# Two phase-weight loads given other landing buffers, and one tile's turn and store moved to other engines, in a chunk-attention and phase-MLP kernel

## The chip, the cores and the metric

The kernel runs on one core of a Trainium2 chip. The metric is the device time of one execution in microseconds (us). Three runs of the kernel before took 190.2, 190.77 and 191.58 us, with a median of 190.77 us. One further execution was profiled, and it took 190.93 us.

## The reference

Eight batches of 576 tokens pass through attention with 8 heads of 64 features, each chunk of 64 tokens attending only to itself. The 512 features of each token then go through a phase layer, a token mix and a channel layer.

```python
scores = scale * np.matmul(q_c, k_c.transpose(0, 1, 2, 4, 3))   # chunks of 64
attn = softmax(scores)
x = np.matmul(attn, v_c)                                        # heads side by side: (8, 576, 512)
theta = x @ w_theta
zr, zi = x * np.cos(theta), x * np.sin(theta)
u = x + np.einsum('ts,bsd->btd', w_tok_r, zr) + np.einsum('ts,bsd->btd', w_tok_i, zi)
out = u + np.maximum(u @ w_ch, 0.0)
```

## The kernel before, in words

The batches are handled in four pairs p = 0 to 3. A batch has 4 full tiles of 128 tokens and a half tile of 64; the two halves of a pair share one tile. So a pair has nine tiles j = 0 to 8, and j = 8, the middle tile (`MID`), holds the last 64 tokens of both batches. Loads and attention go by groups: A and B are the two pairs of tiles of the first batch, C and D those of the second, M is the middle tile.

Nothing plans the order of the work: it is written out by hand in the list `ORDER` (lines 17 to 64), and a loop at the end (lines 640 to 647) issues it step by step. Each engine takes its own instructions of that list strictly in turn. A step reads `kind.pg.slot`: the kind names a function of the table `work` (lines 612 to 639), then come pair and group (or pair and tile), then a buffer or a PSUM bank. Whoever takes a buffer again waits until its former content has been read, by a DMA too: a step that writes an output buffer `o` again waits until the store out of it has landed. The steps that this text speaks of are:

- `hq.0A`, `hk.0A` (`load_qk32`, line 180): q and k of group 0A as 32-bit floats by SP's DMA queue, 512 KB each, into landing buffers 0 and 1. `cqa.0A` on ScalarE (ACT) and `ckv.0A` on VectorE (DVE) cast them into landing buffer 3 (line 192).
- `lt.00`, `lt.01` (`load_theta`, line 252): the two halves of `w_theta`, 512 KB each, also by SP's queue. `cta.01` and `cta.00` (line 261) cast them on ACT. TensorE (PE) needs both before `H0.0A`, the first product with `w_theta`.
- `qk` (line 161) and `v` (line 205): all other loads of q, k and v. They are issued by GpSimd (POOL), which casts them to 16 bits on the way.
- `Tq`, `Tk`, `T` (line 314) turn q and k in 32 x 32 blocks on DVE; `S` and `V` are the products of attention on PE; `E` the exponentials on ACT; `dm.n` are n matmuls of zeros on PE, which fill its waits (line 155).
- `Y` mixes tokens on PE (line 523); `A` adds x on DVE (line 550), which makes u.
- u must be turned before the channel product. `U` does it with four transposes on PE into a PSUM bank (line 554), and `ua` copies the bank into a buffer `uT` on ACT. `ud` does it as one DMA transpose from SP's queue into `uT` (line 565).
- `W` is the channel product on PE (line 575): four matmuls of 512 columns. `R` takes relu and adds u on DVE, into a buffer `o` (line 588).
- Stores of `o` (line 600): `st` from SP's queue, `sa` from ACT's, `sg` from POOL's. A middle tile takes two DMAs of 64 rows, one per batch. `sx` issues the first of these on SP and the second on ACT; the table has it, but `ORDER` before doesn't use it.

Near the end, `ORDER` writes the buffers `o` in this order (the last number is the buffer): `R.35.1 R.31.2 R.34.0 R.30.3 R.36.5 R.33.1 R.27.2 R.32.4 R.38.0 R.24.3 R0.37.1 R1.37.2`. Out of these, ACT stores 35, 34, 33, 27, 24 and the second half of the columns of 37, in that order. So `R.33` waits for the store of 35 (both use `o` 1), `R0.37` for the store of 33 (`o` 1) and `R1.37` for the store of 27 (`o` 2).

Of the kernel before, what the change touches and what calls it, by code (L numbers as in the profile page):

```python
# [19 lines left out]
V1.0A.6 N0.0A S.0M.0 N1.0A cta.01 Tq.0B.2 E.0M.1 v.0M cta.00 dm.6.3 X1.0A.2 Tk0.0B  # L20
X0.0A.3 dm.2.7 S0.0B.4 Tk1.0B V0.0M.0 xa0.0A.0 V1.0M.1 xa1.0A N0.0M E0.0B.2 S1.0B.6
E1.0B H0.0A.3 v.0B V1.0B.4 G0.0A.0 V0.0B.6 lw.01.7 H1.0A.2 N1.0M N1.0B X.0M.0 xa.0M.1
lw.03.8 N0.0B TW.01.4 twv.01 X1.0B.1 X0.0B.3 lw.02.9 xv0.0B.2 lw.00.10 G1.0A Z0.0A Z1.0A
xa1.0B H.0M.6 G.0M.1 H0.0B.7 TW.03.4 G0.0B.2 H1.0B.0 twv.03 G1.0B Z.0M Z0.0B qk.0C.11
Ya.01.3 v.0C Z1.0B TW.02.1 qk.0D.12 Ya.03.6 twa.02 Tq.0C.0 TW.00.4 Ym.05.7 Tk.0C v.0D
Ya.02.0 Yb.02 twv.00 S.0C.1 Ym.02 A.02 Yb.01 E.0C.3 Ym.01 V1.0C.4 A.01 V0.0C.0 Tq.0D.1
N1.0C Yb.03 lc.00 Ya.00.2 U.02.3 Tk.0D Yb.00 Ym.00 S.0D.4 N0.0C ua.02.0 A.00 X.0C.3
U.00.0 U.01.1 Ym.03 E.0D.0 xv.0C.3 uv.01.1 V1.0D.4 ua.00.2 N1.0D V0.0D.2 N0.0D qk.1M.0
qk.1A.1 H.0C.0 v.1M qk.1B.3 A.03 v.1A Ym.06.4 X.0D.5 W.02.2 Ym.07.3 xv.0D.0 G.0C.0 Z.0C
H.0D.5 Ya.05 Ya.06 Ya.07 G.0D.1 T.1M.2 S.1M.0 T.1A.0 Z.0D R.02.0 S.1A.5 E.1A.1 Yb.05  # L30
Yb.06 Ym.04.2 A.05 E.1M.2 V0.1M.5 N0.1M qk.1D.5 V1.1M.6 V1.1A.0 A.06 N1.1M Ya.04 T.1B.1
Yb.07 U.06.7 ua.06.3 A.07 X.1M.5 Yb.04 xa.1M.1 S.1B.6 N1.1A lw.04.4 TW.04.4 twv.04
H.1M.3 A.04 v.1B V0.1A.0 E.1B.3 V1.1B.4 G.1M.2 qk.2A.2 V0.1B.6 N0.1A N0.1B N1.1B Y.08.2
A.08 X.1A.0 W.00.1 U.04.6 qk.1C.6 X.1B.7 xa.1A.2 R.00.1 qk.2M.7 Z.1M T.1D.2 xa.1B.3
qk.2B.8 v.1D U.08.3 ua.08.4 v.2M v.1C ua.04.5 H.1A.4 G.1A.0 st.02 H.1B.0 W.08.2 W.06.7
U.05.3 T.1C.0 S.1D.4 G.1B.1 qk.2C.9 Z.1A Z.1B ua.05.6 E.1D.0 S.1C.0 W.01.6 R.06.2 U.07.3
sa.06 E.1C.2 T.2A.1 ua.07.7 Y.12.7 V1.1D.4 R.01.3 V0.1D.0 Y.13.6 T.2M.2 N0.1D S.2M.0
sa.01 E.2M.1 R.08.4 N1.1D S.2A.2 V1.1C.4 E.2A.3 sa.08 V0.1C.0 A.12 Y.11.7 X.1D.2 xa.1D.0
N1.1C N0.1C X.1C.3 xv.1C.1 Y.10.4 A.13 H.1D.0 qk.3M.10 v.2B T.2C.0 A.11 A.10 T.3M.2
G.1D.2 Z.1D H.1C.2 W.04.5 R.04.5 U.03.6 W.05.7 S.2C.0 v.2A st.00 S.3M.4 uv.03.0 G.1C.0  # L40
Z.1C R.05.0 E.3M.0 v.3M E.2C.2 st.04 V1.2A.2 N1.2A W.03.6 R.03.1 T.2B.1 Y.16.7 A.16
V0.2M.4 N0.2M v.2C V1.2C.2 V1.2M.5 qk.3A.11 N1.2C S.2B.0 N1.2M E.2B.1 qk.2D.12 Y.18.6
V1.3M.7 V0.2C.0 A.18 N0.2C V0.2B.2 N0.2B Y.14.4 V1.2B.5 V0.2A.0 qk.3C.0 v.2D N1.2B
U.18.2 Y.15.3 X.2B.5 A.14 X.2M.6 W.07.4 uv.18.2 xa.2B.2 N0.2A xa.2M.3 A.15 X.2A.2 v.3B
xa.2A.0 H.2B.0 T.3C.0 R.07.2 T.2D.2 G.2B.1 qk.3B.1 W.18.3 R.18.3 H.2A.5 U.15.4 Y.17.2
U.10.3 H.2M.0 Z.2B G.2A.2 ua.15.4 ua.10.3 N1.3M G.2M.0 S.3C.5 Z.2A A.17 S.2D.3 E.2D.2
W.15.1 U.17.7 Z.2M Y.20.2 uv.17.1 V1.2D.3 E.3C.1 A.20 V0.3M.0 V0.2D.5 st.05 Y.23.7
xd.2C.1 N1.2D A.23 N0.2D T.3B.1 U.14.2 U.11.3 sa.18 N0.3M xd.2D.2 W.17.4 ua.11.5 U.16.7
R.15.4 st.07 Y.21.3 A.21 R.17.5 qk.3D.3 v.3C v.3A H.2C.5 ua.16.6 T.3A.0 W.10.7 ua.14.0
G.2C.1 T.3D.2 H.2D.0 G.2D.2 Y.22.2 Z.2C R.10.0 S.3D.3 S.3A.5 st.15 E.3A.3 S.3B.0 E.3D.0  # L50
Z.2D Y.26.7 sg.03 U.12.5 A.22 U.13.2 sa.10 ua.13.7 W.11.6 R.11.3 Y.25.3 A.26 E.3B.2 v.3D
sa.11 ud.23.2 ud.21.4 W.16.4 A.25 R.16.1 W.13.2 V1.3D.0 R.13.2 V1.3A.6 V0.3A.3 N1.3D
ua.12.1 N0.3A st.16 sa.13 xd.3M.0 N1.3A Y.24.5 A.24 Y.27.2 A.27 W.12.0 R.12.4 V0.3D.3
V1.3B.6 V0.3B.1 N1.3B xd.3A.3 ud.20.3 N0.3B N0.3D Y.28.5 V1.3C.6 V0.3C.0 A.28 W.14.2
H.3M.3 G.3M.0 R.14.0 xd.3B.1 ud.25.5 N0.3C H.3A.4 xd.3D.2 G.3A.1 W.21.2 N1.3C R.21.3
W.23.0 Z.3A H.3B.6 G.3B.2 sg.17 Z.3M ud.24.6 W.25.1 sa.21 R.23.5 xd.3C.0 H.3D.2 ud.28.7
W.20.4 H.3C.5 ud.22.1 G.3D.1 R.25.1 Z.3B Y.30.0 G.3C.0 Z.3D ud.26.0 sg.12 Z.3C Y.31.7
R.20.2 A.30 A.31 Y.36.1 Y.35.2 W.22.3 A.35 R.22.4 Y.33.5 W.28.6 A.33 Y.34.4 sg.23 A.34
ud.35.4 R.28.3 ud.31.2 W.26.0 Y.32.7 Y.37.2 W.35.3 A.36 ud.33.5 R.26.5 W.31.5 A.32 A.37
# [618 lines left out]
```

## Time and profile before

| what | value |
|---|---|
| median of three runs | 190.77 us (190.2 to 191.58) |
| the profiled execution | 190.93 us |
| its span, first to last instruction | 189.2 us |
| PE busy | 180.9 us (96%), 2645 matmuls |
| DVE busy | 136.7 us (72%) |
| ACT busy | 94.8 us (50%) |
| POOL busy | 89.5 us (47%) |
| matmuls of zeros (line 157), part of PE's | 51, 14.1 us |
| DMA moved | 31.48 MB, mean 166 GB/s |

Times in the profile count from the span's first instruction. "PE" is TensorE's matmuls and "PEld" its weight loads, which overlap them; "SPq" and "ACTq" are DMAs issued by those engines' queues. In a row of the timeline the first number is the start, the second the duration (of several instructions that follow each other, their common stretch), and brackets tell how long the engine was idle before and what ended that.

### The profile page before, as it was taken

The page shows a single profiled execution, that of the slowest core. Times are in us where ns is not written, and L with a number is a line of the kernel's source. Part 1 is how long each engine was busy: PE and PEld are TensorE (multiplying, and loading weights), DVE is VectorE, ACT ScalarE, POOL GpSimd, SP SyncE. Part 2 cuts the span into 40 slices and gives each one's busy share as a digit, 9 for nine tenths or more (in the row PEclk, how much of TensorE's full clock was granted, in tenths as well). Part 3 has the DMA queues.
Part 4 walks back from the last instruction along what each step waited for, and adds up shares of the span by engine and source line. Part 5 has one row for each costly group of instructions (what it writes and reads, how often), then busy time and mean ns, then how long its engine had stood idle before and what let it go on. Part 6 is the DMA issues. An engine that isn't in the chain of part 4 may idle for free.

```text
span 189.2 us, 6104 instructions
## 1 busy us (share of the span) xinstructions
PE 180.9 (96%) x2645; PEld 93.4 (49%) x2645; DVE 136.7 (72%) x259; ACT 94.8 (50%) x123; POOL 89.5 (47%) x129
## 2 busy tenths in 40 slices
PE   7998999999999999999999999999999999999970
...
GB/s 151 285 194 172 177 167 170 189 168 168 192 194 180 198 126 206 178 101 191 209 166 146 172 214 52 248 60 59 140 153 154 183 177 59 55 110 204 206 317 166
DMA packets 99227, 31.48 MB, mean 166 GB/s; under 512 B 90880, under 2 KB 94848, under 8 KB 99200
## 3 DMA queue, kind: packets, MB, share of 16 engines
...
q1 hardware_dynamic: 20896, 8.92, 21.2%
...
## 4 chain that ended last, share of the span: by engine, by line
PE 74%; DMA 17%; DVE 3%; issue 2%; POOL 2%; SPq 0%; DVEq 0%; POOLq 0%
PE psum L540 34%; PE psum L475 15%; PE psum L580 12%; DMA land<-in_k_dram 9%; PE psum L354 4%; PE psum L400 3%; DMA land<-in_q_dram 3%; DMA uT<-x 3%; PE psum L437 2%; PE psum L557 2%; DMA v<-in_v_dram 2%; PE psum L287 2%; POOL v L213 1%; DVE o L592 1%; DVE T L335 1%
## 5 line engine op out<-in xcount | busy, mean ns | idle before, releaser
L213 POOL DMA_DIRECT2D v<-in_v_dram x56 | 41.7, 765 | 14.5 <-DMA land<-in_k_dram 9.1
L540 PEld LDWEIGHTS <-wT 128*128 128x128 f16 (+1 forms) x360 | 30.6, 100 | 33.4 <-issue 0.8
L540 PE MATMUL psum<-zr,wT 128*128 128x512 f16 (+1 forms) x180 | 45.4, 381 | 0.1
L540 PE MATMUL psum<-zi,wT 128*128 128x512 f16 (+1 forms) x180 | 43.1, 379 | 0.0
L608 POOL DMA_DIRECT2D out_dram<-o x10 | 5.5, 552 | 66.3 <-DVE o L592 46.2
L580 PE MATMUL psum<-wch,uT 128*128 128x512 f16 (+1 forms) x148 | 35.2, 374 | 1.1 <-DMA uT<-x 1.1
L552 DVE TENSOR_TENSOR x<-psum,x 128x512 f16<-128x512 f32 x36 | 24.4, 683 | 15.8 <-PE psum L540 15.1
L475 PE MATMUL psum<-wtheta,xT 128*128 128x512 f16 x144 | 34.1, 379 | 0.0
L592 DVE SCALAR_TENSOR_TENSOR o<-psum,x 128x512 f32<-128x512 f32 (+1 forms) x37 | 24.3, 670 | 10.3 <-PE psum L580 6.2
L494 ACT ACTIVATE cos<-psum,pihalf 128x1024 f16<-128x1024 f32 (+1 forms) x22 | 21.2, 964 | 16.1 <-PE psum L475 16.1
L335 DVE STREAM_TRANSPOSE T<-land 64x256 f32<-64x256 f32 (+3 forms) x38 | 27.0, 725 | 2.6 <-DMA land<-in_k_dram 2.3
L417 DVE TENSOR_TENSOR x<-psum,recip 128x512 f16<-128x512 f32 (+1 forms) x40 | 25.5, 638 | 1.4
L383 ACT ACTIVATE eT<-psum 128x1024 f16<-128x1024 f32 (+1 forms) x22 | 18.4, 864 | 15.8 <-PE psum L354 15.8
L580 PEld LDWEIGHTS <-uT 128*128 128x128 f16 x148 | 13.7, 98 | 16.2 <-DMA uT<-x 1.6
L475 PEld LDWEIGHTS <-xT 128*128 128x128 f16 x144 | 13.5, 98 | 15.3 <-DVE xT L460 0.2
...
L494 ACT ACTIVATE sin<-psum 128x1024 f16<-128x1024 f32 (+1 forms) x22 | 19.1, 870 | 0.0
L173 POOL DMA_DIRECT2D land<-in_q_dram x15 | 13.6, 904 | 4.8 <-DVE recip L415 2.1
L157 PE MATMUL psum<-zeros 128*128 128x512 f16 x51 | 14.1, 436 | 1.2 <-DVE pihalf L148 1.2
L173 POOL DMA_DIRECT2D land<-in_k_dram x15 | 13.5, 902 | 2.0 <-DMA land<-in_k_dram 1.4
L462 ACT COPY xT<-psum 128x512 f16<-128x512 f16 (+1 forms) x11 | 8.4, 784 | 10.4 <-PE psum L437 10.4
L354 PEld LDWEIGHTS <-T 32*64 32x64 f16 x1152 | 10.6, 105 | 5.4 <-DVE T L335 2.1
...
## 6 DMA issues: line engine op xcount, KB each, us to landing
land<-in_q_dram POOLq DMA_DIRECT2D x15, 256.0 KB, 6.8
land<-in_k_dram POOLq DMA_DIRECT2D x15, 256.0 KB, 7.8
out_dram<-o ACTq DMA_DIRECT2D x12, 256.0 KB, 3.2
...
out_dram<-o POOLq DMA_DIRECT2D x10, 256.0 KB, 3.4
out_dram<-o SPq DMA_DIRECT2D x9, 256.0 KB, 3.3
...
```

Source lines behind the costliest of these rows:

```text
L173: nc.gpsimd.dma_start(t[:, w].rearrange("p h s d -> p h (s d)"), ap[2 * p + bb, :, s0 : s0 + GT, :].rearrange("h (p s) d -> p h (s d)", s=2),)
L213: nc.gpsimd.dma_start(v16[rows, slot + t, :, 0:D], v[b, :, t0 : t0 + m, :].rearrange("h s d -> s h d"),)
L335: nc.vector.transpose(to.bitcast(FP32).rearrange("p (x l s) -> p x s l", l=32, s=2), src.bitcast(FP32).rearrange("p (x s d) -> p x s d", s ...
L354: nc.tensor.matmul(ps[half[rows], r, h - hs[0]], t[quarter[c], 1, h, :, e], t[quarter[c], 0, h, :, e], start=(e == 0), stop=(e == 1), tile ...
L383: nc.scalar.activation(out=to, in_=ps, func=AF.Exp, scale=scale)
L417: nc.vector.tensor_tensor(out=x.rearrange("p r (h d) -> p r h d", h=H // 2), in0=ps[:, :, :, 0:D], in1=recip[:, 0:n].broadcast_to((P, n, H ...
L475: nc.tensor.matmul(ps[:, (j - js[0]) * DM : (j - js[0] + 1) * DM], xT[:, j, a, :], wtheta16[:, a, :], start=(a == 0), stop=(a == NDB - 1),)
L494: nc.scalar.activation(out=t[:, js[0] : js[-1] + 1].rearrange("p j e -> p (j e)"), in_=ps, func=AF.Sin, bias=bias, scale=1.0,)
L540: nc.tensor.matmul(ps[half[c]] if j == MID else ps, wT[:, kt, t0 : min(t0 + P, S)], z, start=(b is not None and i == 0), stop=(i == len(kt ...
L552: nc.vector.tensor_tensor(out=x, in0=st.pop(("ps_y", p, j)), in1=x, op=ALU.add)
L580: nc.tensor.matmul(ps, uT[:, a, :], wch16[:, a, cols[f]], start=(a == 0), stop=(a == NDB - 1),)
L592: nc.vector.scalar_tensor_tensor(out=o, in0=ps, scalar=0.0, in1=st["x", p][:, j, cols[f]], op0=ALU.max, op1=ALU.add,)
```

## The change

Only `ORDER` changes. Nothing is added to the functions.

1. `lt.00` goes into landing buffer 0 instead of 2 and stands behind `cqa.0A`; `lt.01` goes into buffer 1 instead of 4 and stands behind `ckv.0A`. Each load therefore waits, on SP's queue, until the cast has read the buffer.
2. The turn of u of tile 38 (the middle tile of the last pair) is `U.38.2 ua.38.3` behind `W.36` instead of the DMA transpose `ud.38.3` behind `ud.37`. In ACT's own queue `ua.38` now stands ahead of `sa.35`, and so of all later stores of ACT.
3. The store of tile 38 is `sx.38` ahead of `W.24` instead of `st.38` behind `R0.37`. Its first half is issued by SP, its second by ACT ahead of `sa.24`.

In the list (lines are wrapped anew from the first changed one on, so the parts are cut out; the code below `ORDER` stands three lines higher afterwards):

```diff
-pre.00 hq.0A.0 hk.0A.1 lt.00.2 cqa.0A.3 ckv.0A Tq.0A.0 init.00 Tk1.0A Tk0.0A dm.28.7
-S0.0A.0 S1.0A.2 lt.01.4 qk.0M.5 E0.0A.0 v.0A dm.15.7 V0.0A.4 E1.0A Tq.0M.1 Tk.0M qk.0B.6
+pre.00 hq.0A.0 hk.0A.1 cqa.0A.3 lt.00.0 ckv.0A lt.01.1 Tq.0A.0 init.00 Tk1.0A Tk0.0A dm.28.7
+S0.0A.0 S1.0A.2 qk.0M.5 E0.0A.0 v.0A dm.15.7 V0.0A.4 E1.0A Tq.0M.1 Tk.0M qk.0B.6 V1.0A.6 N0.0A
 ...
-ud.27.4 sg.14 W.34.6 W.36.1 W.30.0 W.33.7 sg.31 sa.35 R.34.0 ud.37.2 ud.38.3 R.30.3
-st.30 W.27.2 sa.34 R.36.5 sg.22 R.33.1 sg.36 R.27.2 W.32.3 R.32.4 W.38.5 R.38.0 sg.32
-sa.33 sa.27 W.24.4 R.24.3 sa.24 W0.37.6 R0.37.1 st.38 W1.37.0 R1.37.2 sa1.37 st0.37
+ud.27.4 sg.14 W.34.6 W.36.1 U.38.2 ua.38.3 W.30.0 W.33.7
+sg.31 sa.35 R.34.0 ud.37.2 R.30.3 st.30 W.27.2 sa.34 R.36.5 sg.22 R.33.1 sg.36 R.27.2 W.32.3
+R.32.4 W.38.5 R.38.0 sg.32 sa.33 sa.27 sx.38 W.24.4 R.24.3 sa.24 W0.37.6 R0.37.1 W1.37.0 R1.37.2
+sa1.37 st0.37
```

More of the change, by code (lines that the diff above doesn't have):

```diff
@@ L17 @@
 ORDER = """
-pre.00 hq.0A.0 hk.0A.1 lt.00.2 cqa.0A.3 ckv.0A Tq.0A.0 init.00 Tk1.0A Tk0.0A dm.28.7
-S0.0A.0 S1.0A.2 lt.01.4 qk.0M.5 E0.0A.0 v.0A dm.15.7 V0.0A.4 E1.0A Tq.0M.1 Tk.0M qk.0B.6
[L20 to L59, printed above, removed]
@@ L60 @@
-Y.38.4 ud.34.3 ud.30.1 st.26 ud.36.7 sa.20 sg.25 sa.28 R.35.1 R.31.2 ud.32.0 A.38
-ud.27.4 sg.14 W.34.6 W.36.1 W.30.0 W.33.7 sg.31 sa.35 R.34.0 ud.37.2 ud.38.3 R.30.3
-st.30 W.27.2 sa.34 R.36.5 sg.22 R.33.1 sg.36 R.27.2 W.32.3 R.32.4 W.38.5 R.38.0 sg.32
-sa.33 sa.27 W.24.4 R.24.3 sa.24 W0.37.6 R0.37.1 st.38 W1.37.0 R1.37.2 sa1.37 st0.37
+pre.00 hq.0A.0 hk.0A.1 cqa.0A.3 lt.00.0 ckv.0A lt.01.1 Tq.0A.0 init.00 Tk1.0A Tk0.0A dm.28.7
+S0.0A.0 S1.0A.2 qk.0M.5 E0.0A.0 v.0A dm.15.7 V0.0A.4 E1.0A Tq.0M.1 Tk.0M qk.0B.6 V1.0A.6 N0.0A
@@ new lines @@
+S.0M.0 N1.0A cta.01 Tq.0B.2 E.0M.1 v.0M cta.00 dm.6.3 X1.0A.2 Tk0.0B X0.0A.3 dm.2.7 S0.0B.4
+Tk1.0B V0.0M.0 xa0.0A.0 V1.0M.1 xa1.0A N0.0M E0.0B.2 S1.0B.6 E1.0B H0.0A.3 v.0B V1.0B.4 G0.0A.0
+V0.0B.6 lw.01.7 H1.0A.2 N1.0M N1.0B X.0M.0 xa.0M.1 lw.03.8 N0.0B TW.01.4 twv.01 X1.0B.1 X0.0B.3
+lw.02.9 xv0.0B.2 lw.00.10 G1.0A Z0.0A Z1.0A xa1.0B H.0M.6 G.0M.1 H0.0B.7 TW.03.4 G0.0B.2 H1.0B.0
+twv.03 G1.0B Z.0M Z0.0B qk.0C.11 Ya.01.3 v.0C Z1.0B TW.02.1 qk.0D.12 Ya.03.6 twa.02 Tq.0C.0
+TW.00.4 Ym.05.7 Tk.0C v.0D Ya.02.0 Yb.02 twv.00 S.0C.1 Ym.02 A.02 Yb.01 E.0C.3 Ym.01 V1.0C.4
@@ new lines @@
+A.01 V0.0C.0 Tq.0D.1 N1.0C Yb.03 lc.00 Ya.00.2 U.02.3 Tk.0D Yb.00 Ym.00 S.0D.4 N0.0C ua.02.0
+A.00 X.0C.3 U.00.0 U.01.1 Ym.03 E.0D.0 xv.0C.3 uv.01.1 V1.0D.4 ua.00.2 N1.0D V0.0D.2 N0.0D
+qk.1M.0 qk.1A.1 H.0C.0 v.1M qk.1B.3 A.03 v.1A Ym.06.4 X.0D.5 W.02.2 Ym.07.3 xv.0D.0 G.0C.0 Z.0C
+H.0D.5 Ya.05 Ya.06 Ya.07 G.0D.1 T.1M.2 S.1M.0 T.1A.0 Z.0D R.02.0 S.1A.5 E.1A.1 Yb.05 Yb.06
+Ym.04.2 A.05 E.1M.2 V0.1M.5 N0.1M qk.1D.5 V1.1M.6 V1.1A.0 A.06 N1.1M Ya.04 T.1B.1 Yb.07 U.06.7
+ua.06.3 A.07 X.1M.5 Yb.04 xa.1M.1 S.1B.6 N1.1A lw.04.4 TW.04.4 twv.04 H.1M.3 A.04 v.1B V0.1A.0
@@ new lines @@
+E.1B.3 V1.1B.4 G.1M.2 qk.2A.2 V0.1B.6 N0.1A N0.1B N1.1B Y.08.2 A.08 X.1A.0 W.00.1 U.04.6 qk.1C.6
+X.1B.7 xa.1A.2 R.00.1 qk.2M.7 Z.1M T.1D.2 xa.1B.3 qk.2B.8 v.1D U.08.3 ua.08.4 v.2M v.1C ua.04.5
+H.1A.4 G.1A.0 st.02 H.1B.0 W.08.2 W.06.7 U.05.3 T.1C.0 S.1D.4 G.1B.1 qk.2C.9 Z.1A Z.1B ua.05.6
+E.1D.0 S.1C.0 W.01.6 R.06.2 U.07.3 sa.06 E.1C.2 T.2A.1 ua.07.7 Y.12.7 V1.1D.4 R.01.3 V0.1D.0
+Y.13.6 T.2M.2 N0.1D S.2M.0 sa.01 E.2M.1 R.08.4 N1.1D S.2A.2 V1.1C.4 E.2A.3 sa.08 V0.1C.0 A.12
+Y.11.7 X.1D.2 xa.1D.0 N1.1C N0.1C X.1C.3 xv.1C.1 Y.10.4 A.13 H.1D.0 qk.3M.10 v.2B T.2C.0 A.11
@@ new lines @@
+A.10 T.3M.2 G.1D.2 Z.1D H.1C.2 W.04.5 R.04.5 U.03.6 W.05.7 S.2C.0 v.2A st.00 S.3M.4 uv.03.0
+G.1C.0 Z.1C R.05.0 E.3M.0 v.3M E.2C.2 st.04 V1.2A.2 N1.2A W.03.6 R.03.1 T.2B.1 Y.16.7 A.16
+V0.2M.4 N0.2M v.2C V1.2C.2 V1.2M.5 qk.3A.11 N1.2C S.2B.0 N1.2M E.2B.1 qk.2D.12 Y.18.6 V1.3M.7
+V0.2C.0 A.18 N0.2C V0.2B.2 N0.2B Y.14.4 V1.2B.5 V0.2A.0 qk.3C.0 v.2D N1.2B U.18.2 Y.15.3 X.2B.5
+A.14 X.2M.6 W.07.4 uv.18.2 xa.2B.2 N0.2A xa.2M.3 A.15 X.2A.2 v.3B xa.2A.0 H.2B.0 T.3C.0 R.07.2
+T.2D.2 G.2B.1 qk.3B.1 W.18.3 R.18.3 H.2A.5 U.15.4 Y.17.2 U.10.3 H.2M.0 Z.2B G.2A.2 ua.15.4
@@ new lines @@
+ua.10.3 N1.3M G.2M.0 S.3C.5 Z.2A A.17 S.2D.3 E.2D.2 W.15.1 U.17.7 Z.2M Y.20.2 uv.17.1 V1.2D.3
+E.3C.1 A.20 V0.3M.0 V0.2D.5 st.05 Y.23.7 xd.2C.1 N1.2D A.23 N0.2D T.3B.1 U.14.2 U.11.3 sa.18
+N0.3M xd.2D.2 W.17.4 ua.11.5 U.16.7 R.15.4 st.07 Y.21.3 A.21 R.17.5 qk.3D.3 v.3C v.3A H.2C.5
+ua.16.6 T.3A.0 W.10.7 ua.14.0 G.2C.1 T.3D.2 H.2D.0 G.2D.2 Y.22.2 Z.2C R.10.0 S.3D.3 S.3A.5 st.15
+E.3A.3 S.3B.0 E.3D.0 Z.2D Y.26.7 sg.03 U.12.5 A.22 U.13.2 sa.10 ua.13.7 W.11.6 R.11.3 Y.25.3
+A.26 E.3B.2 v.3D sa.11 ud.23.2 ud.21.4 W.16.4 A.25 R.16.1 W.13.2 V1.3D.0 R.13.2 V1.3A.6 V0.3A.3
@@ new lines @@
+N1.3D ua.12.1 N0.3A st.16 sa.13 xd.3M.0 N1.3A Y.24.5 A.24 Y.27.2 A.27 W.12.0 R.12.4 V0.3D.3
+V1.3B.6 V0.3B.1 N1.3B xd.3A.3 ud.20.3 N0.3B N0.3D Y.28.5 V1.3C.6 V0.3C.0 A.28 W.14.2 H.3M.3
+G.3M.0 R.14.0 xd.3B.1 ud.25.5 N0.3C H.3A.4 xd.3D.2 G.3A.1 W.21.2 N1.3C R.21.3 W.23.0 Z.3A H.3B.6
+G.3B.2 sg.17 Z.3M ud.24.6 W.25.1 sa.21 R.23.5 xd.3C.0 H.3D.2 ud.28.7 W.20.4 H.3C.5 ud.22.1
+G.3D.1 R.25.1 Z.3B Y.30.0 G.3C.0 Z.3D ud.26.0 sg.12 Z.3C Y.31.7 R.20.2 A.30 A.31 Y.36.1 Y.35.2
+W.22.3 A.35 R.22.4 Y.33.5 W.28.6 A.33 Y.34.4 sg.23 A.34 ud.35.4 R.28.3 ud.31.2 W.26.0 Y.32.7
```

2 lines of the change are left out of this document (added).

## The prediction

> **What bounds the kernel now.** I read the page first, then PE's waits, the chain, and the timelines of the first 20 and last 20 us.
>
> ```profile
> span 189.2 us, 6104 instructions
> PE 180.9 (96%) x2645; PEld 93.4 (49%) x2645; DVE 136.7 (72%) x259; ACT 94.8 (50%) x123; POOL 89.5 (47%) x129
> ...
> PE   7998999999999999999999999999999999999970
> ...
> L157 PE MATMUL psum<-zeros 128*128 128x512 f16 x51 | 14.1, 436 | 1.2 <-DVE pihalf L148 1.2
> ```
>
> ```profile
> PE psum L157 <- DVE pihalf L148: 1.2, 1, 1.2
> PE psum L580 <- DMA uT<-x: 1.1, 1, 1.1
> PE psum L354 <- DVE T L335: 0.8, 1, 0.8
> ```
>
> The second view lists all waits of PE, each with its total, count and longest. PE waits three times only: 1.2 us at the start, 0.8 us for turned q and k, and 1.1 us for a turned u. From the second wait to the third it runs without a gap, so what comes earlier or later at the front moves everything behind it. The change touches the last two. Their places:
>
> ```profile
> 9.72 0.71 PE L354 MATMUL psum<-T 32*64 32x64 f16 x64
> 10.36 3.41 PE L157 MATMUL psum<-zeros 128*128 128x512 f16 x15
> ...
> 17.66 0.45 PE L354 MATMUL psum<-T 32*64 32x64 f16 x32 [0.81 <-DVE T L335]
> ```
>
> ```profile
> 7.76 9.38 DMA land<-in_k_dram
> 17.14 0.02 issue
> 17.16 0.46 DVE T L335
> ...
> 52.58 0.22 PE psum L557 x4
> ...
> 176.01 5.32 DMA uT<-x
> ```
>
> The first fence is PE's timeline, the second the chain of waits. The wait at 17.66 (`S0.0B`) ends with k of group 0B, which POOL issued at 7.76 and which landed at 17.14. The wait at the end is for `ud.38`, issued at 176.01 and landed at 181.33.
>
> **Part 1, the theta loads.** Cost by the rows, ACT's, DVE's and SP's timeline:
>
> ```profile
> 5.13 1.04 ACT L199 CAST land<-land 128x1024 f16<-128x1024 f32 x1 [2.89 <-DMA land<-in_q_dram]
> ...
> 11.20 1.05 ACT L265 CAST wtheta<-land 128x1024 f16<-128x1024 f32 x1
> 14.59 0.60 ACT L383 ACTIVATE eT<-psum 128x512 f16<-128x512 f32 x1 [2.34 <-PE psum L354]
> 15.09 1.04 ACT L265 CAST wtheta<-land 128x1024 f16<-128x1024 f32 x1
> ```
>
> ```profile
> 7.11 0.69 DVE L201 CAST land<-land 128x1024 f16<-128x1024 f32 x1 [5.32 <-DMA land<-in_k_dram]
> ```
>
> ```profile
> 1.87 1.95 SPq L256 DMA_DIRECT2D land<-in_moe_w_theta_dram  x2
> ```
>
> `lt.00` is issued at about 6.2 (5.13 + 1.04) instead of 1.87, `lt.01` at about 7.85 (7.11 + 0.69) instead of some 3.3. On SP's queue nothing stands behind them until the stores, much later, so the waits there block nobody. The loads of q and k stood ahead of the theta loads in the same queue, so I don't expect them to land earlier. If they did, PE would still work through its 28 matmuls of zeros up to 9.72.
>
> How late may theta be? Landing took 7.5 to 7.7 us where the loads stood behind q and k, while those two, on an empty queue, took 4.4 and 5.8 us:
>
> ```profile
> L256 SPq DMA_DIRECT2D land<-in_moe_w_theta_dram x2: 471/955/1439, 1.9 to 3.3; - x2
> ...
> DMA to landing us min/median/max: 7.5/7.6/7.7
> ```
>
> ```profile
> L185 SPq DMA_DIRECT2D land<-in_q_dram x1: 451/451/451, 0.7 to 0.7; - x1
> L185 SPq DMA_DIRECT2D land<-in_k_dram x1: 567/567/567, 1.3 to 1.3; - x1
> ...
> DMA to landing us min/median/max: 4.4/5.1/5.8
> ```
>
> The queue is nearly empty now, so I take 4.4 to 5.8: `lt.01` lands between 12.3 and 13.7, `cta.01` moves from 11.20 to there and ends by 14.75. Behind it in ACT's queue stands the exponential of 14.59, so this is free within 0.2 us. With 7.7 it would land at 15.55; `cta.01`, the exponential, `cta.00`, two copies (1.07) and the exponentials of 0B would follow one another, and `V1.0B` would start some 0.7 us late. That is the upper bound.
>
> Does k of 0B land earlier? POOL issued it behind seven loads, and its bytes, theta's and those ahead of it must all pass by 17.14 either way. The DMA engines carry as much before 6 us as after:
>
> ```profile
> 3.00:4.00 1.00, 1.00 (x4) 0.34 (x3) 0.00 (x0) 0.00 (x0) 1.00 (x3) 1.00 1.14 345
> ...
> 7.00:8.00 1.00, 1.00 (x6) 0.49 (x5) 0.89 (x2) 0.00 (x0) 0.41 (x2) 1.00 1.14 280
> 8.00:9.00 1.00, 1.00 (x7) 0.41 (x6) 1.00 (x4) 0.00 (x0) 0.64 (x1) 1.00 1.22 321
> ```
>
> (the last two numbers of a row of windows are the DMA engines' share and GB/s). They are full throughout; moving theta 1.5 us later in that stream changes the order, not the sum. So I take 0, between a gain of 0.81 (the whole wait) and a loss of 0.7.
>
> **Part 2, the turn of tile 38.** The tail, PE's, DVE's, ACT's and SP's timelines:
>
> ```profile
> 174.92 5.35 PE L580 MATMUL psum<-wch,uT 128*128 128x512 f16 x24
> 181.37 2.77 PE L580 MATMUL psum<-wch,uT 128*128 128x512 f16 x16 [1.10 <-DMA uT<-x]
> ```
>
> ```profile
> 175.03 0.69 DVE L552 TENSOR_TENSOR x<-psum,x 128x512 f16<-128x512 f32 x1 [1.38 <-PE psum L540]
> ...
> 177.72 3.28 DVE L592 SCALAR_TENSOR_TENSOR o<-psum,x 128x512 f32<-128x512 f32 x5 [1.03 <-PE psum L580]
> 182.45 0.69 DVE L592 SCALAR_TENSOR_TENSOR o<-psum,x 128x512 f32<-128x512 f32 x1 [1.45 <-PE psum L580]
> 183.31 1.35 DVE L592 SCALAR_TENSOR_TENSOR o<-psum,x 128x512 f32<-128x512 f32 x3 [0.17 <-PE psum L580]
> ```
>
> ```profile
> 172.82 12.29 ACTq L608 DMA_DIRECT2D out_dram<-o  x6
> ```
>
> ```profile
> 183.17 1.19 SPq L605 DMA_DIRECT2D out_dram<-o  x2
> 184.46 0.53 SPq L608 DMA_DIRECT2D out_dram<-o  x1
> ```
>
> The 24 matmuls are `W` of 34, 36, 30, 33, 27, 32, the 16 are 38, 24 and both halves of 37. The five of DVE are `R` of 30, 36, 33, 27, 32, some 0.6 apart, so `R.33` starts at about 178.92; then come `R.38` and, in the last row, `R.24`, `R0.37` and `R1.37`, the last starting at 184.25 and ending at 184.66. The six stores of ACT are 35 (at 172.82), 34, 33, 27, 24 and the second half of 37.
>
> PE gains the 1.10 us and pays 0.22 (four transposes, as at 52.58 in the chain): W of 38 starts at about 180.4, and PE ends at 183.2 instead of 184.14, 0.9 us earlier. `A.38` ends at 175.72, before `U.38` can start (`W.36` leaves PE at 174.92 + 8 x 0.216 = 176.65), and `ud.37`, due at 182.1, landed at 180.02. By PE alone this part gains 0.9.
>
> But `ua.38` is queued on ACT ahead of `sa.35`. A copy of this kind took:
>
> ```profile
> L569 ACT COPY uT<-psum x2: 586/586/586, 128.1 to 130.1; 128x512 f16<-128x512 f16 x2
> ```
>
> The four transposes have left PE at about 177.03, the copy lasts until 177.66, and `sa.35` is issued at about 177.75 instead of 172.82: 4.9 us later. `sa.34` follows it, and its reader `R.38` is not due before 181.5. `R.33`, however, writes the buffer out of which `sa.35` stores, and may start only when that has landed; behind it on DVE stand `R.27`, `R.32`, `R.38`, `R.24` and both halves of `R.37`. And these take buffers again themselves: `R1.37` waits for the store of `R.27`. With d for a store's time from issue to landing, `R.33` starts at 177.80 + d; `R.27` 0.60 later, ends 0.68 later still; `sa.27` is issued 0.03 behind, lands after d, and `R1.37` starts 0.05 later. The sum: `R1.37` starts at 179.16 + 2d. The rows for d:
>
> ```profile
> out_dram<-o ACTq DMA_DIRECT2D x12, 256.0 KB, 3.2
> ```
>
> ```profile
> L608 ACTq DMA_DIRECT2D out_dram<-o x6: 338/338/413, 172.8 to 184.7; - x6
> ...
> DMA to landing us min/median/max: 2.6/3.3/4.4
> ```
>
> The first is the median of all of ACT's stores of this size, the second the six at the end alone. With 3.2, `R.33` starts at 181.0 (2.1 us late), and `R1.37` at 185.56 instead of 184.25: 1.3 us later. With 2.6 it is 184.36 (0.1 later), with 4.4 it would be 187.96 (3.7 later). I take 3.2, because the stores around the same moment (issued from 176.7 to 180.6) had 3.4 and 4.4, but with two DMA transposes beside them, one of which goes.
>
> [...]
>
> **Part 3, the store of 38 in halves.** SP issued two DMAs in 1.19 us, so `st0.37` went out at 184.46, 0.1 behind them. Now one leaves from each queue, and earlier than `R0.37`. `st0.37` then goes directly behind its `R0.37`, at 185.0 + 0.4 by the sum above, ahead of `sa1.37`, which stays last. ACT's extra issue (0.34 in the rows of ACT's stores) comes before `R1.37` ends, so it is free. With the stores of 38 and 24 out of the way over 1 us ahead of the last one I give it 0.2 us back of its landing; between 0 and the distance from 3.3 to 2.6, that is 0.7.
>
> **The sum.** 0 at the front, +1.3 by the reuse of `o`, -0.2 at the last landing: +1.1 us. The profiled execution took 190.93 us, 1.7 more than its span of 189.2; so 192.0 for it. Its time stands 0.16 above the median of the three runs, which makes 191.9 us against 190.77.
>
> **The rivals.**
>
> *Faster, because stores land quickly.* `R1.37` starts earlier than before if 179.16 + 2d is below 184.25, that is with d below 2.55. For it speaks that `ud.38` no longer competes and that `sa.35` is the first of a new burst; against it that five of the six rows lie above and none below 2.6. With 2.4 the tail gains 0.3, and 190.5 comes out. Should nobody wait for `o` at all, PE's 0.9 would count: 189.9.
>
> *Slow landings.* With `sa.35`, `sa.34` and the stores of SP and POOL leaving within 2 us, d may be as in the worst row, 4.4: 3.7 later, 194.5 us. For it: the two rows of 4.4 and 3.4 at this very moment.
>
> *The front pays.* If k of 0B lands 0.8 earlier, `S0.0B` doesn't wait, and all behind it gains 0.81: 191.1. If theta is the later one, 0.7 is lost: 192.6. Neither changes the sign.
>
> *The change doesn't do what it says.* With d at 2.6 PE's gain and the new wait cancel out: 190.9.
>
> **How the numbers follow.** The forecast (d of 2.8 to 3.7) has 0.53, the fast landings 0.12, the cancelling 0.17, slow landings 0.18; the front shifts each by up to 0.8 and is as likely either way. The predicted time is 191.9; its own range is 191.0 to 193.0. The range for 8 of 10 leaves out half of the fast case and the worst of the slow one: 190.3 to 193.6. Within 1% is 188.9 to 192.7, about what a measurement of this kernel can tell from no change. Faster by more takes the whole of PE's gain and the front's together: 0.04. Slower by more takes d above 3.6 or a loss at the front: 0.25. The rest, 0.71, is within 1%.
>
> **What would show it.** Right: the copy of tile 38 on ACT at about 177.1 with `sa.35` directly behind it, a wait of about 2 us of DVE ahead of the third of the five `R`, released by a store; PE's wait of 1.1 us gone and PE done near 183.2; `R1.37` starting near 185.5; the wait of 0.8 at 17.66 still there. Wrong: DVE not waiting for a store in the tail, `sa.35` issued before the copy, a wait of ACT or PE for theta before 20 us, or `S0.0B` without its wait.

## The result, and the profile after

The kernel after took 192.16 us as the median of nine executions (191.69 to 193.9), the kernel before, measured beside it, 190.77 us, also the median of nine (190.2 to 191.58). The ratio is 1.009, with a 95% interval of 1.0063 to 1.0117: 1.2 to 2.2 us slower. The prediction of 191.9 us (190.3 to 193.6) was right in its number. Its sum was not: it put all of the loss, +1.1, at the end of the program and nothing at the front. Both ends cost, and by other terms than the forecast's.

The profiled execution of the kernel after is the longest of its nine: 193.9 us, span 192.1 us; the other spans lie between 189.9 and 191.0. So a second execution of the same kernel, profiled in experiment 10 at 192.44 us, stands beside it wherever a number matters. Ratios leave out single executions that were over 1.5% longer than the fastest of their kernel, and in experiment 6 that is the profiled one (193.87 us). In the kernel after, the code has line numbers three lower than before.

The page of the kernel after: span, engines, and PE's granted clock in 40 equal slices of the span.

```profile
span 192.1 us, 6115 instructions
...
PE 182.6 (95%) x2649; PEld 94.0 (49%) x2649; DVE 136.6 (71%) x259; ACT 95.3 (50%) x124; POOL 89.6 (47%) x129
...
PEclk9999699999999999999999999999999999999998
```

PE has the four transposes more, 1.7 us more busy time, and in the fifth slice (19.2 to 24.0 us) a clock of only 0.6. PE's waits, of this execution and then of experiment 10 (same kernel):

```profile
PE psum L351 <- DVE T L332: 1.4, 1, 1.4
PE psum L154 <- DVE pihalf L145: 1.2, 1, 1.2
PE psum L537 <- issue: 0.3, 1, 0.3
PE psum L472 <- ACT xT L459: 0.2, 1, 0.2
```

```profile
PE psum L154 <- DVE pihalf L145: 1.2, 1, 1.2
PE psum L351 <- DVE T L332: 1.1, 1, 1.1
PE psum L537 <- issue: 0.7, 1, 0.7
PE psum L397 <- ACT eT L380: 0.4, 1, 0.4
PE psum L472 <- ACT xT L459: 0.2, 1, 0.2
```

The wait for `ud.38` (1.1 us before) is gone, as forecast. New are waits for ACT at the front (`H0.0A` for a copied x, `V` of 0B for an exponential) and an "issue" of 0.3 and 0.7 us, which is time in which PE waited for nothing that the profile shows.

**The front.** ACT's timeline of experiment 10:

```profile
9.80 1.08 ACT L380 ACTIVATE eT<-psum 128x512 f16<-128x512 f32 x2 [3.59 <-PE psum L351]
16.04 1.04 ACT L262 CAST wtheta<-land 128x1024 f16<-128x1024 f32 x1 [5.16 <-DMA land<-in_moe_w_theta_dram]
17.00 0.59 ACT L380 ACTIVATE eT<-psum 128x512 f16<-128x512 f32 x1
17.49 1.03 ACT L262 CAST wtheta<-land 128x1024 f16<-128x1024 f32 x1
18.42 1.07 ACT L459 COPY xT<-psum 128x512 f16<-128x512 f16 x2
19.38 1.10 ACT L380 ACTIVATE eT<-psum 128x512 f16<-128x512 f32 x2
```

From 16.04 ACT runs without a gap. The first cast of theta starts 4.84 us later than before (11.20), and the exponential behind it, ready for PE's results at 14.59 before, starts at 17.00. The two theta loads themselves, in the kernel after and in experiment 10 (first and last issue, then from issue to landing):

```profile
L253 SPq DMA_DIRECT2D land<-in_moe_w_theta_dram x2: 368/368/368, 6.2 to 8.1; - x2
...
DMA to landing us min/median/max: 5.9/7.3/8.7
```

```profile
L253 SPq DMA_DIRECT2D land<-in_moe_w_theta_dram x2: 367/368/368, 6.2 to 7.8; - x2
...
DMA to landing us min/median/max: 5.6/6.9/8.2
```

The issues are where the prediction had them; `lt.01` landed at 16.9 (8.1 + 8.7) and 16.0 (7.8 + 8.2) instead of 12.3 to 13.7. Part of the reason stands in the windows of the kernel after (DMA share and GB/s are the last two numbers):

```profile
7.00:8.00 1.00, 1.00 (x6) 0.42 (x5) 0.61 (x1) 0.00 (x0) 0.16 (x1) 1.00 2.09 164
8.00:9.00 1.00, 1.00 (x6) 0.49 (x5) 1.00 (x4) 0.00 (x0) 0.97 (x2) 1.00 2.42 158
```

In the same two windows of the kernel before, quoted in the prediction, 280 and 321 GB/s moved. The DMA engines are "full" in both, with shares over 1 (2.09 and 2.42; before 1.14 and 1.22), but of other packets. The queues between 6 and 8 us, after and then before (packets, MB, share):

```profile
DMA packets 1672, 0.35 MB, mean 174 GB/s; under 512 B 1622, under 2 KB 1672, under 8 KB 1672
...
q0 software_dynamic: 1614, 0.32, 186.3%
q1 hardware_dynamic: 58, 0.03, 5.6%
```

```profile
DMA packets 697, 0.52 MB, mean 262 GB/s; under 512 B 477, under 2 KB 503, under 8 KB 697
...
q1 hardware_dynamic: 226, 0.41, 73.6%
q0 software_dynamic: 471, 0.11, 57.8%
```

Before, SP's packets (`q1`: 226 with 0.41 MB, some 1.8 KB each, nearly all of theta) ran among POOL's small ones (`q0`: 471 with 0.11 MB, some 240 bytes each). After, POOL's ran almost alone and both together moved 174 GB/s; theta was issued late into that, and nearly all of its bytes moved between 9 and 16 us (`q1`: 0.37 MB from 9.5 to 11, 0.41 from 12.5 to 14). The kernel before has such a stretch too, later, when theta has landed:

```profile
11.00:12.00 1.00, 1.00 (x6) 0.49 (x5) 0.49 (x2) 1.00 (x2) 0.82 (x2) 1.00 2.39 153
```

These thin windows alone don't make `lt.01` late. In experiment 5 below, the windows from 7 to 9 us carry 161 GB/s each, and yet `lt.01`, issued at 6.4, landed at 13.0. In experiment 10 it was issued at 7.8, behind POOL's load of q of 0B (6.2), and from 11 to 12 us SP's queue moved next to nothing while POOL's small packets passed:

```profile
q0 software_dynamic: 691, 0.18, 176.6%
q1 hardware_dynamic: 10, 0.02, 4.7%
```

So the later issue of `lt.01` behind POOL's next loads goes with the late landing. That this order is the cause is argued; no run changes it alone.

Of the two stretches from 6 to 8 us, the one with more small packets had the lower rate: 174 GB/s where 1622 of 1672 packets lie below 512 bytes, and 262 where 477 of 697 do.

**The tail.** PE's, ACT's and DVE's timeline of the kernel after:

```profile
177.57 1.90 PE L577 MATMUL psum<-wch,uT 128*128 128x512 f16 x8
179.31 0.39 PE L554 MATMUL psum<-id,x 128*128 128x128 f16 x4
179.53 6.22 PE L577 MATMUL psum<-wch,uT 128*128 128x512 f16 x32
```

```profile
179.73 0.58 ACT L566 COPY uT<-psum 128x512 f16<-128x512 f16 x1 [21.95 <-PE psum L554]
179.79 4.77 ACTq L605 DMA_DIRECT2D out_dram<-o  x4
```

```profile
180.60 1.29 DVE L589 SCALAR_TENSOR_TENSOR o<-psum,x 128x512 f32<-128x512 f32 x2 [1.26 <-PE psum L577]
182.91 3.97 DVE L589 SCALAR_TENSOR_TENSOR o<-psum,x 128x512 f32<-128x512 f32 x7 [1.02 <-DMA out_dram<-o]
```

`W.34` starts 2.65 us later than before (177.57 against 174.92), so all times of the tail are counted from there below. PE runs through. `sa.35` goes out at 2.22 instead of before `W.34`, and DVE waits 1.02 us for it ahead of the third of the five `R`, as forecast. Yet behind that wait, the seven `R` follow one another, and `R1.37` starts at 8.88 instead of 9.33: earlier, not 1.3 later.

The last store of ACT, after and then before (start, and from issue to landing), and the waits of SP at the very end, after and before:

```profile
L605 ACTq DMA_DIRECT2D out_dram<-o x1: 381/381/381, 186.9 to 186.9; - x1
...
DMA to landing us min/median/max: 3.5/3.5/3.5
```

```profile
L608 ACTq DMA_DIRECT2D out_dram<-o x1: 413/413/413, 184.7 to 184.7; - x1
...
DMA to landing us min/median/max: 3.3/3.3/3.3
```

```profile
L670 SPq EVENT_SEMAPHORE  x2: 28/28/28, 190.4 to 190.9; - x2
```

```profile
L673 SPq EVENT_SEMAPHORE  x5: 28/28/28, 188.0 to 188.3; - x5
```

After, the last store landed at 190.4 and the span ended at 192.1: 1.7 us. Before, it landed at 188.0 and the span ended at 189.2: 1.2 us. In those last microseconds SP passes one wait after another for stores that have landed. Before, five of them took 0.3 us; after, SP needs 0.5 us for one step from one to the next (190.4 to 190.9). No row of the prediction looked at this place.

### The profile page after: what moved, and what is told of

Same layout as the page of the kernel before. It is cut to its first block, busy times and chain, and to the rows that moved or that the text cites. A ratio compares the mean times of both kernels' runs of the same rounds, so it can differ in the third digit from the quotient of the medians.

```text
span 192.1 us, 6115 instructions
## 1 busy us (share of the span) xinstructions
PE 182.6 (95%) x2649; PEld 94.0 (49%) x2649; DVE 136.6 (71%) x259; ACT 95.3 (50%) x124; POOL 89.6 (47%) x129
## 4 chain that ended last, share of the span: by engine, by line
PE 78%; DMA 9%; DVE 6%; issue 2%; ACT 1%; SPq 0%; ACTq 0%; DVEq 0%
PE psum L537 37%; PE psum L472 15%; PE psum L577 12%; DMA land<-in_moe_w_theta_dram 5%; PE psum L351 4%; PE psum L397 4%; DMA land<-in_k_dram 3%; PE psum L434 3%; DVE o L589 2%; PE psum L554 2%; DMA out_dram<-o 2%; PE psum L284 2%; DVE T L332 1%; DVE x L549 1%; DVE zi L508 1%
## 5 line engine op out<-in xcount | busy, mean ns | idle before, releaser
L472 PE MATMUL psum<-wtheta,xT 128*128 128x512 f16 x144 | 35.4, 390 | 0.2 <-ACT xT L459 0.2
L566 ACT COPY uT<-psum 128x512 f16<-128x512 f16 x15 | 8.5, 592 | 32.5 <-PE psum L554 31.5
L472 PEld LDWEIGHTS <-xT 128*128 128x128 f16 x144 | 13.7, 100 | 16.1 <-issue 1.1
L577 PEld LDWEIGHTS <-uT 128*128 128x128 f16 x148 | 13.8, 98 | 14.6 <-issue 0.4
L170 POOL DMA_DIRECT2D land<-in_q_dram x15 | 13.7, 915 | 4.0 <-DVE recip L412 2.0
L170 POOL DMA_DIRECT2D land<-in_k_dram x15 | 13.7, 912 | 2.9 <-DMA land<-in_k_dram 2.0
```

The lines of the kernel that those rows point to most:

```text
L170: nc.gpsimd.dma_start(t[:, w].rearrange("p h s d -> p h (s d)"), ap[2 * p + bb, :, s0 : s0 + GT, :].rearrange("h (p s) d -> p h (s d)", s=2),)
L472: nc.tensor.matmul(ps[:, (j - js[0]) * DM : (j - js[0] + 1) * DM], xT[:, j, a, :], wtheta16[:, a, :], start=(a == 0), stop=(a == NDB - 1),)
L577: nc.tensor.matmul(ps, uT[:, a, :], wch16[:, a, cols[f]], start=(a == 0), stop=(a == NDB - 1),)
```

## The experiments

Theory: part 1 makes theta late and ACT late behind it, and part 2 pays for the reuse of `o`. Rivals: part 1 is free; the turn costs by something other than the reuse; the difference is chance. All edits are to `ORDER` of the kernel before, whose line numbers they keep, and each ratio is against runs of the kernel before on the same chip. A ratio comes from the single executions of both kernels, so it need not be the quotient of the two medians: in experiment 1 that quotient is 1.002, the ratio 1.004.

**1. Part 1 alone.**

```diff
-lt.00.2 cqa.0A.3 ckv.0A
+cqa.0A.3 lt.00.0 ckv.0A lt.01.1
 ...
-lt.01.4
```

> Part 1 alone: the two theta loads wait for the casts and take landing buffers 0 and 1; the tail is that of before. Theory of the prediction: the DMA engines carry the same bytes either way, so 0 (190.6 to 191.0 us). Theory after the trace of the changed kernel: k of 0B lands 0.7 us later and the first product with w_theta starts 1.0 us later, so about +1.0 (191.6 to 192.0 us), nearly all of the change's loss. S0.0B then starts near 18.4 instead of 17.66.

Measured: 191.56 us against 191.16, ratio 1.0043 (1.0016 to 1.007): 0.3 to 1.3 us. The front costs, where the prediction had 0. Its profile shows a mild execution: `lt.01` landed at 14.6, just in time.

```profile
14.61 1.04 ACT L265 CAST wtheta<-land 128x1024 f16<-128x1024 f32 x1 [3.53 <-DMA land<-in_moe_w_theta_dram]
```

PE waits for ACT nowhere in it, and `H0.0A` starts at 18.84 (before: 18.89). `S0.0B` starts at 17.71, not near 18.4 as the theory after the trace had it. Up to 30 us PE loses nothing, and yet `W.34` starts 1.11 us late: PE stands still at 39 and at 93 us (0.22 and 0.69 us, "issue"), which the first profile of the kernel before doesn't have (last section). So the size is measured, but this profile doesn't show the cause, and the standstills are a rival to ACT's wait.

**2. Parts 2 and 3 alone.**

```diff
-W.34.6 W.36.1 W.30.0
+W.34.6 W.36.1 U.38.2 ua.38.3 W.30.0
 ...
-ud.38.3
 ...
-sa.33 sa.27 W.24.4 R.24.3 sa.24 W0.37.6 R0.37.1 st.38
+sa.33 sa.27 sx.38 W.24.4 R.24.3 sa.24 W0.37.6 R0.37.1
```

> Parts 2 and 3 alone: tile 38 turned on PE and copied on ACT ahead of store 35, its store in halves; the theta loads are those of before. Theory of the prediction: R.33 waits for the late store and R1.37 starts 1.3 us later, so +1.1 (191.5 to 192.3 us). Theory after the trace: stores land in 2.1 to 3.0 us at this place, R1.37 starts up to 0.5 us earlier and the last landing takes it back, so -0.4 to +0.3 (190.4 to 191.1 us). In both DVE waits about 1 us or more for a store ahead of R.33.

Measured: 191.57 against 191.16, ratio 1.0029 (1.0006 to 1.0052): 0.1 to 1.0 us, where the prediction had 1.1 and the theory after the trace 0.3 at most. DVE waits as in the kernel after:

```profile
180.01 3.97 DVE L592 SCALAR_TENSOR_TENSOR o<-psum,x 128x512 f32<-128x512 f32 x7 [1.08 <-DMA out_dram<-o]
```

The product of the ratios of experiments 1 and 2 is 1.0072, inside the interval of the whole change: the two ends add up.

**3. The same, but the store of 35 stays ahead of the copy on ACT.** This takes away what DVE waits for.

```diff
-U.38.2 ua.38.3 W.30.0 W.33.7 sg.31 sa.35
+sa.35 U.38.2 ua.38.3 W.30.0 W.33.7 sg.31
```

> As the tail alone, but with store 35 ahead of U and copy of tile 38 in ACT's queue, so that R.33 finds its buffer free. If the reuse of o is what costs (the prediction), this takes the whole 2 us of R.33's wait away and leaves PE's gain: about -0.9 against before (189.7 to 190.1 us), and 1 to 2 us less than the tail alone. If stores land so fast that the wait is nearly paid for (after the trace), it is only 0.3 to 0.5 us less than the tail alone. No wait of DVE for a store ahead of R.33 in either.

Measured: 191.47 against 191.16, ratio 1.004 (1.0012 to 1.0068). DVE's wait for a store is gone, and the five `R` are one group again:

```profile
178.65 3.28 DVE L592 SCALAR_TENSOR_TENSOR o<-psum,x 128x512 f32<-128x512 f32 x5 [1.26 <-PE psum L580]
```

`R1.37` starts at 8.41 (experiment 2: 8.93) from the start of `W.34`, and the span ends at 13.86 (14.64). Yet the medians don't differ (191.47 and 191.57), and the kernel stays 0.2 to 1.3 us slower than before, where the prediction's theory had it 0.9 faster. So the wait that the prediction built on costs 0.5 us of `R1.37` in the trace, which these medians can neither show nor rule out; it is not where the loss sits.

**4. Part 3 alone** (`sx.38` behind `sa.27`, no `st.38`; the DMA transpose stays).

```diff
-sa.27 W.24.4 R.24.3 sa.24 W0.37.6 R0.37.1 st.38
+sa.27 sx.38 W.24.4 R.24.3 sa.24 W0.37.6 R0.37.1
```

> Part 3 alone: before, with the store of tile 38 issued in halves by SP and ACT behind R.38 instead of by SP behind R0.37; the turn stays the DMA transpose. Prediction: 0.0 to -0.3 us (190.4 to 190.8), as R1.37 and its store end last as before. Rival: two queues for one tile only share the same engines, so nothing at all, and ACT's last store leaves up to 0.4 us later behind one more issue: up to +0.3.

Measured: 190.83 against 191.16, ratio 0.9988 (0.9958 to 1.0017). The halves by themselves change nothing that can be measured; the -0.2 us of the prediction fits.

**5. Only `lt.00` moved** (into buffer 0 behind `cqa.0A`; `lt.01` keeps buffer 4).

```diff
-lt.00.2 cqa.0A.3
+cqa.0A.3 lt.00.0
```

> Of part 1 only the first load: lt.00 waits for the cast of q and takes landing buffer 0; lt.01 is issued early into buffer 4, as before. It is then issued behind lt.00 in SP's queue all the same, so both leave at about 6.2 us instead of 1.9 and 3.3. If the front's loss comes from the DMA engines standing partly idle between k's end and theta's start (part 1 alone: +0.4%), half to all of it stays: 191.3 to 191.9 against 191.0 of before. If it comes from lt.01 alone, which waited for the cast of k, nothing stays: 190.8 to 191.2.

**6. Part 1, with the two casts exchanged,** so that ACT waits for the load that was issued first.

```diff
-cta.01 Tq.0B.2 E.0M.1 v.0M cta.00
+cta.00 Tq.0B.2 E.0M.1 v.0M cta.01
```

> Part 1 in full, but ACT casts the half of w_theta that lands first (cta.00) ahead of the exponential of 0M, and cta.01 behind it. If the loss comes from ACT, which stood 3.5 to 5.5 us in front of cta.01 for a load that landed last, it goes: 0 against before (within 0.2%). If it comes from k of 0B, which lands later, it stays as in part 1 alone: +0.3 to +0.5%.

Measured, on one chip: ratios of 1.0018 (0.9987 to 1.0049) and 1.0014 (0.9986 to 1.0041), both against 190.78 us. In the first `lt.01` landed at 13.03. In the second it landed at 16.29, as late as after the change, but the exponential stood ahead of its cast:

```profile
14.45 0.60 ACT L383 ACTIVATE eT<-psum 128x512 f16<-128x512 f32 x1 [1.55 <-PE psum L354]
16.31 1.04 ACT L265 CAST wtheta<-land 128x1024 f16<-128x1024 f32 x1 [1.26 <-DMA land<-in_moe_w_theta_dram]
```

Neither made PE wait for ACT, and neither is measurably slower than before. That agrees with ACT's wait as the price of part 1. It doesn't prove it, since both intervals overlap that of experiment 1, and no run separates ACT's wait from PE's standstills.

**7. The turn alone** (part 2, with `st.38` as before).

```diff
-W.34.6 W.36.1 W.30.0
+W.34.6 W.36.1 U.38.2 ua.38.3 W.30.0
 ...
-ud.38.3
```

> Part 2 alone: tile 38 turned on PE and copied on ACT ahead of store 35; its store stays whole on SP behind R0.37. Theory of the prediction: R1.37 1.3 us later, and so +1.1 us or more. Theory after the tail alone: R1.37 up to 0.4 us earlier, its store lands 0.2 later; SP's walk through the waits at the program's end either stands still for 0.45 us as in the tail alone (then +0.2 to +0.6 us), or does not, if that belongs to the number of SP's instructions (then -0.4 to +0.1).

Measured: 192.45 against 190.78, ratio 1.0075 (1.0051 to 1.01). By itself the turn costs 1.0 to 1.9 us, and with the halves beside it (experiment 2) less than half of that. That is the size that the prediction's theory had, but not its mechanism, as `R1.37` starts at 8.81 from `W.34`, between the two executions of the kernel before (table below). The tails of the traces don't show so much either: from the start of `W.34` the span ends at 14.81 here and at 14.64 there. Ahead of `W.34` this trace is 1.40 us behind that of experiment 2, and 1.2 of that arises at PE's two standstills (0.22 and 0.95 us, against 0.12 and none). Whether they were as long in the other executions is not known, so the difference stays unexplained.

**8. Experiment 3, and the store of 34 from SP's queue.**

```diff
-R.34.0 ud.37.2 R.30.3 st.30 W.27.2 sa.34
+R.34.0 ud.37.2 st.34 R.30.3 st.30 W.27.2
```

> Candidate for better than before: tile 38 turned on PE, store 35 ahead of its copy in ACT's queue, the store of 34 issued by SP, 38 in halves, theta as before. No wait of DVE for a store ahead of R.33, R1.37 0.9 us earlier by PE's gain. If SP's standstill of 0.45 us at the program's end goes with the one more instruction on SP: -0.6 to -0.9 us against before. If it stays: -0.1 to -0.5.

Measured: 191.87 against 190.78, ratio 1.0051 (1.0028 to 1.0074). Taking one store more off ACT gains nothing, and the gain that both theories expected did not come. Its last store lands at 12.25 from the start of `W.34`, between the two executions of the kernel before (table below), so what it loses in the tail comes after the last landing.

**9. The kernel before again, and 10. the kernel after again.**

> The kernel before against itself: how far medians and single profiles of one and the same program differ. The ratio should hold 1 within 0.3%. In the profiles so far TensorE stood 0 to 1.9 us near 92 us for nothing but its own instructions, in kernels with and without the change; if that is chance, this profile may have it too (before's first one had none), and k of 0B lands between 16.7 and 17.3 us. If it comes with the change, PE has no idle time there.

> The changed kernel again. The sum of its parts, measured alone (+0.4% and +0.3%), gives +0.7%; its first measurement gave +0.9%. The half-speed clock of 3.4 us behind the wait at 18.4 us, which its first profile had in the slowest of nine runs, should be absent (mean clock 0.99 instead of 0.987), the wait of R.33 for a store of 1.0 to 1.7 us present, and the time from the last landing to the end 1.7 us as in all kernels that turn tile 38 on PE.

Measured on one chip, against 190.76 us: 191.13, ratio 1.0017 (0.9993 to 1.0041), and 192.49, ratio 1.0092 (1.0061 to 1.0123). The loss repeats in this second measurement, and equal code comes out equal. The profile of 9 has PE's standstills too (0.15 and 0.16 us), so they don't come with the change. In that of 10 the clock is not halved (0.997), and `R.33` waits 0.6 us, less than the 1.0 to 1.7 expected. The profile of 9 has no wait for `ud.38` at all. In the six profiled executions of kernels that have `ud.38`, that wait was 0, 0.35, 0.59, 1.0, 1.1 and 1.3 us: PE's gain of 0.9 was read from one of the larger ones. In these kernels `R1.37` starts 8.2 to 8.3 us behind `W.34` plus this wait.

**11. and 12. Stores moved to SP's queue,** so that SP has as many instructions as before: 11 is experiment 8 with `st.36` for `sg.36`; 12 is experiment 3 with

```diff
-sg.36
+st.36
 ...
-sg.32
+st.32
```

> As the candidate with 35 ahead and 34 on SP, with the store of 36 on SP as well, which brings SP's program to as many instructions as before (93; the kernels with the turn on PE had 89 to 92 and took 1.7 us from the last landing to the end, those with 92 and 93 and no turn 1.17). If the number of SP's instructions decides, 1.17 us and -0.6 to -1.0 us against before in all. If it comes with the turn on PE, 1.7 us and -0.3 to +0.5.

> The other way to the same number of SP's instructions (93): store 35 ahead of the copy of tile 38, 34 on ACT as in the change, 36 and 32 on SP instead of POOL. The two theories give the same as for the kernel with 34 and 36 on SP: 1.17 us from the last landing to the end and -0.6 to -1.0 us if SP's number of instructions decides, 1.7 us and -0.3 to +0.5 if the turn on PE does.

Measured: 190.72 and 190.63 against 190.76, ratios 0.9993 (0.9962 to 1.0025) and 0.9987 (0.996 to 1.0014). Both have the turn on PE, and the loss is gone. The gain of 0.6 to 1.0 us, expected if SP's number of instructions decides, did not come. The last store of experiment 12:

```profile
L608 ACTq DMA_DIRECT2D out_dram<-o x1: 338/338/338, 184.8 to 184.8; - x1
...
DMA to landing us min/median/max: 3.1/3.1/3.1
```

It landed at 187.9, and the span ended at 189.0, 1.1 us later. The tails together (times from the start of `W.34`; the last column counts SP's instructions in the trace):

| kernel | `R1.37` starts | last landing | end of span | landing to end | SP |
|---|---|---|---|---|---|
| before | 9.33 | 13.07 | 14.24 | 1.17 | 91 |
| before again (9) | 8.27 | 11.78 | 12.94 | 1.17 | 91 |
| 1 | 9.53 | 13.24 | 14.40 | 1.16 | 93 |
| 5 | 9.23 | 12.97 | 14.14 | 1.17 | 92 |
| after | 8.88 | 12.82 | 14.53 | 1.70 | 89 |
| after again (10) | 8.47 | 12.27 | 13.95 | 1.68 | 89 |
| 2 | 8.93 | 12.91 | 14.64 | 1.73 | 87 |
| 3 | 8.41 | 12.12 | 13.86 | 1.74 | 87 |
| 7 | 8.81 | 13.03 | 14.81 | 1.78 | 88 |
| 8 | 8.42 | 12.25 | 13.95 | 1.70 | 89 |
| 4 | 8.82 | 12.50 | 13.68 | 1.18 | 90 |
| 11 | 8.28 | 11.99 | 13.17 | 1.18 | 91 |
| 12 | 8.28 | 11.84 | 12.95 | 1.11 | 91 |

In all six executions with 87 to 89 instructions SP stands still for some 0.5 us between its 79th and its 80th, wherever that falls among the last waits. With 90 or more, the 80th is issued while stores are still under way. The turn takes three instructions out of SP's program, the halves one (part 1 adds two), and so this place slides behind the last landing. That it is SP's count and not the turn is shown by 11 and 12: 11 differs from 8 only in `st.36` for `sg.36`, and its time from landing to end falls from 1.70 to 1.18. They moved stores from POOL's queue to SP's as well, so not all of the 1.0 us between experiments 3 and 12 need come from the end.

None of these versions beats the kernel before beyond its interval.

## Why the prediction was right in its number and wrong in its sum

**The waits found.** PE's wait for `ud.38` went, `W.36` and the four transposes ran without a gap, the copy of 38 came at 2.16 from `W.34` (forecast: 177.1, which is 2.2), and DVE waited for the store of 35 ahead of `R.33`. Each was named ahead of time; DVE's wait was about 2 us in the forecast and 1.02 and 0.6 us in the two executions. A sign of being wrong that the prediction named came true as well: ACT waited for theta, until 16.88 and 16.04.

**Part 1, "0 at the front": failed.** The step was "They are full throughout; moving theta 1.5 us later in that stream changes the order, not the sum", and with it 4.4 to 5.8 us for a theta load. A share of busy time is not a rate: the engines carried 164 and 158 GB/s where they had carried 280 and 321, the loads took 5.6 to 8.7 us, and `lt.01` landed 2.3 and 3.2 us later than the latest time of the forecast (13.7), 0.5 and 1.3 later than its upper bound (15.55). The windows that the prediction showed end at 9 us; the one from 11 to 12 (153 GB/s, above) would have told that engines that are full can carry half as much (321 GB/s from 8 to 9 us). Why `lt.01` was so late is in part open (result, above). How far behind the kernel before the same matmul of PE ran, in us (the column heads give its time before):

| kernel | `S0.0B`, 17.7 | 30.1 | 90.0 | `W.34`, 174.9 |
|---|---|---|---|---|
| after | 0.70 | 2.32 | 2.18 | 2.65 |
| after again (10) | -0.12 | 0.86 | 0.77 | 1.65 |
| part 1 alone (1) | 0.05 | -0.05 | 0.23 | 1.11 |
| before again (9) | -0.17 | -0.17 | 0.03 | 0.38 |

In experiment 10 PE loses 0.98 us between the first two columns, and 0.73 of that is waiting for ACT (0.20, 0.43 and 0.10), which is what the prediction gave as its upper bound, by the same chain of cast, exponential, cast, copies. In the kernel after, k of 0B landed 0.7 later, ACT cost 0.3, and 1.47 came from the clock (below), of which it regained 0.15. The wait at 17.66 stayed, as forecast (1.4 and 1.1 us). Experiment 1 puts part 1 at +0.8 over many executions. Its own profile lost nothing at the front, where `lt.01` landed at 14.6, and its 1.11 arose at PE's standstills. So that ACT's wait is what part 1 costs is seen in the traces of the kernel after and of experiment 10 and agrees with experiments 5 and 6; that it makes up the whole 0.8 is not shown.

**Part 2, the sizes: failed.** "`sa.35` is issued at about 177.75", behind the end of the copy: it was issued 0.06 us behind the copy's start, 0.6 earlier. "With 3.2" for d: the first store of the burst took 2.99 us (2.56 in experiment 10), but `sa.27`, for which `R1.37` waits, took 2.1, as did `sa.33`:

```profile
L605 ACTq DMA_DIRECT2D out_dram<-o x2: 338/338/338, 183.6 to 184.2; - x2
...
DMA to landing us min/median/max: 2.1/2.1/2.1
```

The sum 179.16 + 2d takes one landing of each kind. Their mean is 2.55 in the kernel after and 2.34 in experiment 10 (2.56 and 2.12), at and below the prediction's own turning point of 2.55, and `sa.35` went out 0.6 earlier besides. So `R1.37` came earlier than 9.33: the rival of the fast landings was right about this place. The rows by which d was chosen (issued from 176.7 to 180.6) are of stores with a DMA transpose beside them; `sa.33` and `sa.27` left at 183.6 and 184.2, when the last transpose had landed (182.1). That this made them faster is not shown: the two stores of ACT before that left behind the last transpose (184.0 and 184.7, behind 181.33) took 3.1 and 3.3 us. The +1.3 of this step was about -0.3: `R1.37` starts at 8.77, the mean of after, after again, 2 and 7, against 9.09, that of before, before again, 1 and 5, which differ among themselves by up to 1.3.

**What took its place.** The tail still cost. Means from `W.34`, of after, after again and 2 against before, before again, 1 and 5: the last landing comes at 12.67 against 12.77, and the end of the span at 14.37 against 13.93. So all of the loss lies behind the last landing, 1.70 us against 1.17. The prediction took the end of the program as a constant.

**Part 3, -0.2:** experiment 4 has -0.2 us with an interval of -0.8 to +0.3.

So +1.1 at the tail and 0 at the front were about +0.5 and +0.8. The sum came out because two errors had opposite signs, which is luck.
